# Linear attention and a mixture of experts on one core: paired x blocks, moved weight loads, split output queues and a new front order

## The chip, the core and the metric

The kernel runs on one core of a Trainium2 chip. A core has five engines with instruction streams of their own: TensorE (PE) multiplies matrices, VectorE (DVE) and ScalarE (ACT) do elementwise work and empty PSUM, GpSimd (POOL) does a little elementwise work, and SyncE (SP) issues DMAs. DMAs are issued from the streams of SP, ACT and POOL, each a queue of its own. Every engine works through its instructions in the order in which they were written, so an instruction that waits holds all behind it. The metric is the device time of one execution in microseconds, lower is better; the result is the median of several runs.

## The reference

```
phi(x) = elu(x) + 1
kv  = einsum('bhsd,bhse->bhde', phi(k), v);  z = sum_s phi(k)
att = (phi(q) @ kv) / (phi(q) . z + 1e-6)          # 8 batches, 8 heads, 576 x 64, float32
x   = att as [4608, 512]                           # tokens x (heads * 64)
P   = exp(x @ w_gate - max), then 8 rounds of normalising rows and columns   # 4608 x 8 experts
out = sum over e of P[:, e] * (relu(x @ w1[e]) @ w2[e])     # w1: 512 x 1024, w2: 1024 x 512
```

Every token goes through all eight experts, so the experts make most of the work. The weights and inputs are float32 in memory; the kernel computes in float16 with float32 sums.

## The kernel before, in words

**Attention.** There are 16 attention steps, numbered n = 2b + g: batch b, and half g of its heads (`att`, L361 on). Each loads k, q and v (L382), each 576 KB of float32: k as float32 (and the very first q), the other q and all v as float16. ScalarE takes exponentials (L393, L456), VectorE makes phi with two passes each (L397, L401, L459, L463). PE makes kv (L422), transposes q (L448), and multiplies for denominator and numerator (L479). ScalarE takes the logarithm of the denominator and the exponential of minus that (L492, L497), VectorE multiplies and writes `xT` (L507). The k loads share three buffers with the first q. With `sp` true a load goes to SP's queue: in the kernel before, these are k of n = 0, k of n = 1 and q of n = 0; all the other loads go to POOL's.

**Expert 0** follows behind the attention while it runs. Tokens are cut in nine blocks ("units") of 512. Layer 1 of the first units is plain (`layer1`, L696), layer 2 too (L979); later units use a scheme of seven products for a 2 x 2 split instead of eight, which needs sums of the weights' quarters (`combos`: W at L1021, T at L1035) and of the inputs' quarters (S, L1066).

**x blocks.** For experts 1 to 7 the seven input quarters and their sums are written to memory once (`xd`, `x_blocks`) and read back for every expert (`x_load`, L783) to ten slots `xs`. The units are grouped in `SUBS`: unit 0 is single, then come four pairs. A pair's block has 256 KB, a single unit's 128 KB; in the kernel before each block takes a slot of its own. Seven slots exist from the closing of the front on, the other three only when xT's space is given up (`f_xclose`), after the last reader of `xT` and after the gate's P is done. The order of loading is that of `ORD`: blocks 1, 5, 6, 3, 2, 7, 4.

**Experts 1 to 7** run as 63 steps, each half a pair's layer 1 or all of unit 0's (`l1_half`, `pair`, L801) beside the layer 2 of an earlier unit (`layer2`, L1095). VectorE and, for one group in seven, ScalarE and GpSimd add P times the result to `acc` (L1126, L1133, L1136). PSUM banks are few, so PE waits for these evictions when they are late.

**Weights** come through POOL's queue (`load_w`, L313), with two buffers each for w1 and w2: expert 0's in two pieces (`parts=2`), the others' w1 as two DMAs of 512 KB and w2 as one of 1 MB. A limit of eight outstanding loads is kept on that queue (`p_sw`).

**The end.** For expert 7, `out_dma` (L956) writes each finished tile of 128 tokens as two halves of 64 partitions. Unit 8 is done by `last`, with its own order of tiles.

**What sets the order.** All instructions are recorded as tasks with costs, dependencies, priorities and buffer groups (`_Plan.add`). `_Plan.run` then goes through a simulated time and writes them out engine by engine. `_FRONT` fixes the first part by hand: a list of task numbers with a letter for the engine (p PE, a ACT, d DVE, g POOL, s SP, m a DMA under way, n none), from the start until some way into expert 1's share; after it the planner picks by earliest start and priority. At the beginning 46 warm-up matmuls (L598) stand in PE's stream between the first useful ones.

Of the kernel before, what the change touches and what calls it, by code (L numbers as in the profile page):

```python
# [17 lines left out]
class _Plan:  # L18
# [35 lines left out]
    def run(self):  # L54
# [33 lines left out]
        while left:  # L88
            best = None
            if fixed:  # L90
                t, e = fixed.pop()
                t = self.t[t]
# [3 lines left out]
            for e, lst in avail.items() if best is None else ():  # L96
                te = None
                for t in lst:
                    r = slot(t)
                    if r is None:  # L100
                        continue
                    s = at(e, t, r)
                    if te is None or s < te:
                        te = s
                if te is None:
                    continue
                pick = None
                for t in lst:
                    r = slot(t)
                    if r is not None and at(e, t, r) <= te + 1e-9 and (pick is None or (t["prio"], t["id"]) < (pick["prio"], pick["id"])):  # L110
                        pick = t
                if best is None or te < best[0]:
                    best = (te, e, pick)
# [26 lines left out]
1n 2p 3p 4p 0g 80g 5p 52g 6p 48s 49m 7p 8p 9p 10p 11p 12p 13p 14p 15p 16p 17p 76s 50s  # L140
51m 18p 19p 54a 20p 21p 22p 61n 23p 108n 78g 24p 25p 26p 27p 28p 29p 30p 31p 55d 62a 56d 63d 64d
65p 77m 82a 83d 84d 66a 53m 57n 58p 59a 60a 32p 33p 34p 35p 36p 79m 89n 90a 91d 67p 68a 81m 595n
85n 86p 92d 120g 118g 119m 37p 122g 148g 146g 109g 38p 87a 88d 121m 125d 69p 70a 71a 123m 39p 93p 94d 111g
40p 41p 74p 75d 42p 149m 124a 126d 150g 174g 176g 95p 96a 43p 44p 72p 45p 110m 73d 147m 127n 131n 133d 132a
159n 46p 97p 47p 98a 99a 113n 134d 202g 178g 128p 112m 114g 151m 206g 175m 160a 129d 161d 130d 135p 136d 177m 187n
596p 597p 100p 116g 101d 137p 138a 162d 179m 115m 207m 203m 598p 599p 139p 140a 102p 153d 103d 152a 154d 155n 141a 204g
205m 232g 106g 234g 233m 235m 163p 164a 600p 602p 604p 601d 603d 104g 605d 117m 156p 157a 606p 608p 158d 181d 144p 145d
180a 182d 236g 609a 165p 188a 166a 105m 237m 610p 607a 142p 143d 260g 261m 612p 167p 189d 190d 168a 169a 613d 183n 184p
185d 186d 191p 192d 611a 618p 172p 173d 262g 614p 615d 193p 194a 208a 170p 171d 107m 245n 263m 209d 210d 215n 217d 211n
632n 216a 616p 195p 633p 196a 634d 635p 636a 197a 246a 238a 218d 212p 213d 214d 637p 638d 219p 220d 200p 639p 292g 290g  # L150
247d 248d 201d 239d 240d 221p 222a 291m 641p 640a 642a 264g 617p 223p 293m 224a 225a 265m 198p 199d 624d 267d 241n 619p
249p 250d 273n 266a 242p 243a 244d 626a 620p 643p 320g 294g 318g 346g 274a 268d 275d 276d 348g 322g 321m 251p 252a 303n
226p 621p 644a 297d 227d 253p 622p 645p 319m 349m 296a 254a 228p 304a 646a 229d 298d 305d 269n 230p 270p 231a 271d 255a
277p 350g 376g 295m 278d 272a 374g 323m 375m 377m 331n 332a 333d 406g 647p 648a 258p 259d 666p 279p 280a 628a 256p 306d
257d 623p 281p 282a 283a 299n 665n 300p 630d 307p 301d 308d 378g 302d 324a 667a 347m 379m 359n 351m 360a 325d 361d 334d
668p 651p 309p 310a 284p 285d 326d 362d 669a 670p 653p 311p 312a 286p 287d 327n 654p 380a 335p 336d 328p 661a 313a 329d
330a 288p 289a 381d 560d 404g 407m 405m 493g 671d 353d 652p 352a 408g 460g 494m 314p 315d 337p 659a 338a 561d 672p 674p
675d 673a 339p 316p 354d 317d 355n 387n 389d 388a 491g 382d 390d 676p 678p 409m 461m 469s 462g 340a 677a 492m 463m 341a
470s 356p 363p 364d 464g 465m 471s 500s 417n 357a 679a 358a 501s 680p 410a 342p 343d 365p 366a 649p 562d 419d 344p 345d
553d 367p 368a 418a 681a 699p 383n 384p 385a 411d 386d 554d 369a 495g 496m 502s 563s 432g 433m 434g 435m 655p 391p 392a  # L160
372p 373d 412d 701p 656p 370p 371d 420d 497a 393p 394a 445n 413n 650p 414p 698n 700a 436g 415d 498d 499d 416d 702a 657a
395p 503g 396a 564m 555d 556s 558s 397a 663a 438a 437m 703p 682p 421p 400p 705p 684p 422d 439d 423p 704a 424a 401d 446a
447d 440d 574d 575d 557m 685p 398p 399d 683p 576d 577s 578m 559m 441n 476n 477a 425p 706d 426a 707p 708a 448d 692d 442p
443a 444a 709p 449p 478d 690d 450d 427a 508n 509a 479d 567d 688p 689p 451p 710a 428p 429d 581d 568d 582d 452a 569d 570s
572s 565s 571m 566m 686p 711p 453p 696a 454a 455a 466a 430p 431d 583d 713p 584s 579s 585m 588g 589n 480p 481d 510d 504n
592n 573m 687p 456p 457d 511d 712d 402p 505p 739n 403a 506a 593g 714d 507a 694d 467d 468d 512p 740p 590g 458p 459d 472n
741a 580m 513a 742p 744p 591m 514p 515a 473p 735d 474d 475d 736d 516p 517a 518a 719p 720p 482p 483a 743a 519p 520d 727d
721p 484p 485a 521p 745d 522d 737d 746p 722p 486a 747a 489p 715p 490d 738d 487p 488d 551n 731d 778d 1009s 1011s 748p 749a
729a 750p 752p 751a 779d 732d 780d 523p 524a 754p 552p 716p 733d 526d 753a 755a 786p 717p 723a 787a 525n 527p 586s 1013s
1015s 781s 800p 718p 790p 756d 734d 792p 785n 1017s 725a 791a 1010m 587m 788p 793a 801a 789a 760p 761a 836d 757d 837d 758d  # L170
528d 838d 783s 1019s 1021s 839s 796p 529d 759d 784m 804p 805a 806p 807a 766p 767a 782m 794p 802p 803a 810p 795d 797d 811d
762p 763a 840m 1022m 1014m 808p 809d 1001d 770p 771d 768p 530p 1002d 769d 531d 798p 812p 799a 813a 772p 773a 844p 845a 764p
894d 814d 846p 847a 848p 850p 858p 852p 843n 849a 859a 765a 851a 532d 815d 816d 820p 860p 818p 861a 866p 895d 853d 817d
819a 864p 854p 865a 533p 896d 897s 855d 867d 534d 824p 825a 868p 869d 862p 863a 535d 856p 857a 821a 828p 829d 870p 871a
902p 903a 826p 822p 952d 872d 827d 953d 1003d 823a 954d 955s 1012m 1018m 956m 873d 1004d 906p 830p 831a 908p 916p 876p 841s
899s 957s 909a 912p 536p 874d 537d 918p 901n 907a 875d 917a 922p 920p 594m 878p 898m 877a 919a 921a 904p 905a 923a 882p
883a 880p 881a 879a 926p 924p 538d 886p 913d 914p 927d 925d 887d 915a 910p 539p 540d 911d 884p 960p 961a 888p 889a 928p
962p 963a 959n 966p 964p 541d 885d 929a 930d 967a 965a 968p 969d 542p 543d 974p 975a 934p 970p 978p 976p 931d 971d 1020m
1016m 958m 980p 935a 977a 979a 981a 940p 972p 973a 936p 984p 544d 545p 982p 941a 932d 546d 983d 1023p 1024a 938p 985d 1025p
547d 1029p 986p 944p 937a 939a 1026a 945d 1030a 1031p 1027p 842m 900m 987a 548p 1033p 946p 947a 1028a 933d 942p 549d 1034d 1035p  # L180
1037p 1038a 988p 550d 1000n 625a 1036a 1032d 1513n 943d 1005d 1006d 1051s 1053s 1055s 1057s 1052m 1039p 989p 1043p 1054m 1514g 1056m 990p
1040a 629a 1044a 691d 1045p 1041p 996d 1047p 1065p 1048d 1042a 693d 1059s 1066a 631a 1061s 1060m 1058m 1062m 1063s 1147s 1149s 1064m 1067p
991p 1068a 1046d 1049p 992p 1071p 1072a 1073p 1069p 1074d 1075p 1050a 951a 1076d 774d 997d 1121d 1070a 993p 1077p 1079p 1081p 1078a 695d
1080a 1082a 994p 1085p 1087p 1083p 1086a 627a 1007d 1122d 728a 1084a 1089p 1088d 1123d 1090d 998d 1093p 1094a 1095p 1148m 1096a 1515m 995p
999a 1091p 1092a 1099p 1101p 1097p 1008d 1100a 1124d 1102d 1125p 1126a 1127p 1129d 1128d 1130p 1103p 1104d 1133a 1134g 1098a 1135p 1138p 1151s
1152m 1516n 1150m 1136d 1137d 1105p 1106a 1107p 1109p 1108a 1110a 1153s 1155s 1154m 1141p 1142d 1143d 1113p 1115p 1114a 1139d 1111p 1117p 1161p
1163p 1144p 834d 1116d 1118d 1119p 1157s 1131a 1112a 1156m 1162a 1167p 660a 1159s 1140d 662d 1146d 1145d 1269s 1271s 1164a 1169p 1165p 1120a
1189d 1168a 1193p 1195p 891a 1158m 1190d 1191d 1194a 664a 1198p 1201a 1166a 892a 658a 1171p 697d 1203p 1160m 1202g 1197d 1196d 1192d 1206p
1172d 1173p 1132g 1199a 1519d 1200g 1175p 1177p 1204d 1205d 1174a 1176a 1209p 1181p 1178a 1183p 1179p 1207d 1517g 1170d 1211d 1208d 1210d 1182a
# [27 lines left out]
def kernel(  # L217
# [553 lines left out]

    xst_of, xse_done, sx_users = {}, [], []

    n_load = [0]

    def x_load(d, blk, prio):
        gr = S_.grp(p_xs)
# [533 lines left out]
```

## Time and profile before

| | us |
|---|---|
| median of 3 runs | 959.46 (959.14 to 959.91) |
| profiled execution | 959.16 |
| its span in the trace | 957.4 |
| PE busy | 945.6 |
| DVE busy | 774.1 |
| ACT busy | 581.8 |
| POOL busy | 146.3 |
| granted PE clock, share of full | 0.999 |
| DMA busy, mean of 16 engines, 0 to 22.4 us | 1.03 of the window |
| the same, 120 to 183 us | 0.49 |
| the same, 183 to 190 us | 0.96 |

Times are counted from the span's start. A line of instructions has start, duration, engine, line of the kernel, operation, and output and inputs by the program's names; in brackets stands how long the engine was idle before it and what released it. SPq, ACTq and POOLq are DMA issues. A wait line has the waiting engine and operation, the releaser, the total, the number and the longest. The chain that ended last follows the work back from the last instruction; its lines have start, duration and what ran. The end of a matmul is modelled, and neighbours overlap, so two matmuls are told apart by their starts.

### The profile page before, as it was taken

To read this page: it belongs to the slowest core of one execution; us is meant where nothing else is said; L and a number is where in the kernel's file an instruction comes from. 1 tells how busy PE (TensorE), PEld (TensorE's weight loads), DVE (VectorE), ACT (ScalarE), POOL (GpSimd) and SP (SyncE) were. 2 spreads that over 40 slices of the span, in tenths; PEclk is the share of its full clock that TensorE was granted. 3 is DMA by queue.
4 is the path that set the end of the run, shared out by engine and by line. 5 is a ranking of instruction groups with operands and counts; after the bars stand their busy time and mean duration, and the time that the engine had idled before them with its cause. 6 is when DMAs were issued, how large, how long until landed. Compare 5 with 4: busy or idle time off the path is not lost.

```text
span 957.4 us, 18335 instructions
## 1 busy us (share of the span) xinstructions
PE 945.6 (99%) x7008; PEld 651.5 (68%) x7008; DVE 774.1 (81%) x1499; ACT 581.8 (61%) x1034; POOL 146.3 (15%) x208
## 2 busy tenths in 40 slices
PE   8999999999999999999999999999999999999997
PEld 4565588666677666766677666766667666776665
DVE  6998999778987888778888888878887888877775
ACT  6899766676655555555555555555555555555552
POOL 6432000001111111111111111111112111111110
PEclk9999999999999999999999999999999999999999
DMA  9998663525136222652217321552217422125544
GB/s 246 262 238 208 157 163 95 154 78 122 61 75 147 77 79 61 176 121 77 63 48 163 89 78 61 139 115 71 76 49 170 116 79 61 56 78 165 165 134 132
DMA packets 87908, 112.65 MB, mean 118 GB/s; under 512 B 7436, under 2 KB 51468, under 8 KB 87820
## 3 DMA queue, kind: packets, MB, share of 16 engines
q1 hardware_dynamic: 63708, 76.77, 26.0%
q0 software_dynamic: 23712, 34.19, 19.2%
q8 instruction: 55, 0.90, 0.4%
q10 hardware_dynamic: 400, 0.52, 0.2%
q14 instruction: 33, 0.27, 0.1%
HBM read 119.69 MB, written 17.69 MB: 143 GB/s over the span
## 4 chain that ended last, share of the span: by engine, by line
PE 90%; DMA 4%; ACT 3%; DVE 2%; issue 1%; SPq 0%; POOL 0%; DVEq 0%
PE ye L1095 36%; PE hq L801 24%; PE R L801 12%; PE Zye L801 6%; PE Zye L1095 6%; PE ye L979 2%; PE hq L696 1%; DMA hb<-in_q_dram 1%; DMA w<-in_moe_w_dram 1%; DMA kin<-in_q_dram 1%; ACT eq L456 1%; DMA xs<-xd 1%; ACT rden L492 1%; PE kv_ps L422 1%; DVE xT L507 0%
## 5 line engine op out<-in xcount | busy, mean ns | idle before, releaser
L1126 DVE SCALAR_TENSOR_TENSOR acc<-ye,P_sb,acc 128x256 f32<-128x256 f32 x620 | 267.2, 479 | 126.6 <-PE ye L1095 124.5
L1095 PEld LDWEIGHTS <-S 128*128 128x128 f16 x1984 | 194.0, 98 | 46.6 <-DVE S L1066 0.2
L1095 PE MATMUL ye<-T,S 128*128 128x256 f16 x1488 | 192.8, 273 | 0.0
L1136 POOL TENSOR_TENSOR acc<-acc,st 128x256 f32<-128x256 f32 x124 | 88.9, 737 | 632.7 <-ACT st L1133 632.7
L1095 PEld LDWEIGHTS <-hb 128*128 128x128 f16 x1584 | 155.0, 98 | 42.7 <-issue 0.8
L801 PEld LDWEIGHTS <-W 128*128 128x128 f16 x1248 | 122.1, 98 | 86.8
L832 ACT ACTIVATE hb<-hq 128x512 f16<-128x512 f32 x134 | 80.0, 597 | 138.6 <-PE hq L801 133.8
L801 PE MATMUL hq<-xs,W 128*128 128x512 f16 (+1 forms) x560 | 150.0, 358 | 0.0
L801 PE MATMUL R<-xs,W 128*128 128x512 f16 (+1 forms) x560 | 150.0, 358 | 0.0
L801 PE MATMUL hq<-xs,w 128*128 128x512 f16 (+1 forms) x560 | 139.8, 358 | 1.3 <-DMA xs<-xd 1.3
L801 PEld LDWEIGHTS <-w 128*128 128x128 f16 x936 | 91.5, 98 | 60.9 <-issue 1.8
L829 ACT ACTIVATE hb<-Zye 128x512 f16<-128x512 f32 x134 | 80.1, 598 | 37.9 <-PE Zye L801 37.8
L835 DVE CUSTOM_DVE_ANT_0 hb<-hq,sx 128x512 f16<-128x512 f32 x126 | 86.6, 687 | 16.8 <-PE hq L801 16.8
L1133 ACT ACTIVATE st<-Zye,P_sb 128x256 f32<-128x256 f32 x124 | 52.5, 471 | 75.6 <-PE Zye L1095 75.6
L822 ACT COPY sx<-hq 128x512 f32<-128x512 f32 x126 | 73.6, 584 | 37.1 <-PE hq L801 37.1
L835 DVE CUSTOM_DVE_ANT_0 hb<-R,sx 128x512 f16<-128x512 f32 x126 | 86.4, 685 | 8.9 <-ACT sx L822 8.9
L818 ACT COPY Zye<-hq 128x512 f32<-128x512 f32 x134 | 77.8, 581 | 21.0 <-PE hq L801 20.8
L1066 DVE TENSOR_TENSOR S<-hb 128x1024 f16<-128x1024 f16 x124 | 84.9, 685 | 4.8 <-ACT hb L832 4.7
L801 PE MATMUL Zye<-xs,w 128*128 128x512 f16 (+1 forms) x280 | 75.0, 358 | 0.0
L826 ACT COPY sx<-R 128x512 f32<-128x512 f32 x126 | 74.4, 591 | 0.0
L1095 PE MATMUL ye<-w,hb 128*128 128x256 f16 x528 | 68.4, 273 | 0.5 <-DVE acc L1126 0.5
L1095 PE MATMUL Zye<-w,hb 128*128 128x256 f16 x528 | 68.4, 273 | 0.0
(119 smaller groups left out, 981.4 us busy)
## 6 DMA issues: line engine op xcount, KB each, us to landing
xs<-xd SPq DMA_DIRECT2D x196, 256.0 KB, 3.8
out_dram<-acc SPq DMA_DIRECT2D x67, 128.0 KB, 2.4
w<-in_moe_w_dram POOLq DMA_DIRECT2D x16, 512.0 KB, 7.9
kin<-in_k_dram POOLq DMA_DIRECT2D x14, 576.0 KB, 8.2
w<-in_moe_w_dram POOLq DMA_DIRECT2D x7, 1024.0 KB, 9.6
xs<-xd SPq DMA_DIRECT2D x49, 128.0 KB, 2.6
vv<-in_v_dram POOLq DMA_DIRECT2D x16, 288.0 KB, 7.2
hb<-in_q_dram POOLq DMA_DIRECT2D x15, 288.0 KB, 7.8
```

What stands on the lines that cost most here:

```text
L801: nc.tensor.matmul(dst_[:, p, :] if parts == 2 else dst_.rearrange("p a b -> p (a b)"), lhsT=lhs(p, c), rhs=blk[i](c), start=(first and p ...
L818: nc.scalar.copy(out=Zt[1], in_=gX["tile"])
L822: nc.scalar.copy(out=gs2["tile"], in_=gX["tile"])
L826: nc.scalar.copy(out=gs5["tile"], in_=gR["tile"])
L829: nc.scalar.activation(out=dst(0, 0), in_=Zt[1], func=AF.Relu)
L832: nc.scalar.activation(out=dst(1, 0), in_=gX["tile"], func=AF.Relu)
L835: nc.vector._custom_dve(TENSOR_ADD_SAT, out=out_, in0=ps, in1=sb, s0=3.0e38, s1=0.0)
L1066: nc.vector.tensor_tensor(out=Sx[:, i], in0=a0, in1=a1, op=op)
L1095: nc.tensor.matmul(bank(g_)[:, s, :], lhsT=lhs(s, kk), rhs=rhs(kk), start=(new and s == 0 and kk == 0), stop=(kk == 3), skip_group_check=True)
L1126: nc.vector.scalar_tensor_tensor(out=dst(), in0=bank(g_)[:, s, :], scalar=P_sb[:, gg, e:e + 1], in1=dst(), op0=ALU.mult, op1=ALU.add)
L1133: nc.scalar.mul(out=gst["tile"], in_=bank(g_)[:, s, :], mul=P_sb[:, gg, e:e + 1])
L1136: nc.gpsimd.tensor_tensor(out=dst(), in0=dst(), in1=gst["tile"], op=ALU.add)
```

## The change

1. A single unit's x blocks go two to a slot, so that its seven blocks take four slots; a paired unit's still take one each.
2. Expert 2's w1 waits in the plan for the x loads of step 1 (the first pair's, for expert 1) to have landed.
3. Only n = 0's k and q go to SP's queue, q first; k of n = 1 goes to POOL's.
4. For unit 7 as well as unit 8, the second half of each output tile is issued by ScalarE and not by SP.
5. In the planner, DMA tasks are picked by readiness and not by priority, and some DMA costs are changed.
6. `_FRONT` is a new list up to task 1842. Among other things, 27 warm-up matmuls and not 30 stand before the first useful one, w1 of expert 0 is loaded in two places (after k of n = 3, and after v of n = 3), and on POOL w1 of expert 1 comes before its w2. From PE's 1,611th matmul on, PE's order is the same in both kernels.

```diff
-                    if r is not None and at(e, t, r) <= te + 1e-9 and (pick is None or (t["prio"], t["id"]) < (pick["prio"], pick["id"])):
+                    if r is not None and at(e, t, r) <= te + 1e-9 and (
+                            pick is None or (t["ready"] if e == "dma" else t["prio"], t["id"]) <
+                            (pick["ready"] if e == "dma" else pick["prio"], pick["id"])):
...
-1n 2p 3p 4p 0g 80g 5p 52g 6p 48s 49m 7p 8p 9p 10p 11p 12p 13p 14p 15p 16p 17p 76s 50s
-51m 18p 19p 54a 20p 21p 22p 61n 23p 108n 78g 24p 25p 26p 27p 28p 29p 30p 31p 55d 62a 56d 63d 64d
+50s 51m 108n 61n 1n 113n 2p 48s 49m 3p 4p 5p 6p 7p 8p 9p 10p 11p 12p 13p 14p 15p 16p 17p
+18p 62a 63d 54a 0g 19p 20p 21p 22p 23p 24p 25p 26p 27p 64d 55d 28p 65p 78g 79m 89n 52g 53m 56d
...
-            sp = wide and b == 0
+            sp = n == 0 and wide
...
-    def x_load(d, blk, prio):
-        gr = S_.grp(p_xs)
-        i = n_load[0] % NXS
-        n_load[0] += 1
-
-        def fn(_):
-            gr["tile"] = xs_t[i]
-            nc.sync.dma_start(out=xs_t[i][:, :, 0:len(SUBS[d])], in_=xd[d][:, blk])
+    def x_load(d, prio):
+        gx = {}
+        dbl = len(SUBS[d]) == 2
+        for m, (blk, b) in enumerate(ORD.items()):
+            h_ = 0 if dbl else m % 2
+            if h_ == 0:
+                gr = S_.grp(p_xs)
+                i = n_load[0] % NXS
+                n_load[0] += 1
+
+            def fn(_, gr=gr, h_=h_, i=i, b=b):
+                gr["tile"] = xs_t[i]
+                nc.sync.dma_start(out=xs_t[i] if dbl else xs_t[i][:, h_], in_=xd[d][:, b] if dbl else xd[d][:, b, :, 0])
...
-            st["x"] = {i: x_load(d, b, un) for i, b in ORD.items()}
+            st["x"] = x_load(d, un)
+            if n == 1:
+                first_x.extend(t for _, t, _ in st["x"].values())
...
-                eng = nc.scalar if g == NG - 1 and half == 1 else nc.sync
+                eng = nc.scalar if g >= NG - 2 and half == 1 else nc.sync
...
-                w_t[e] = load_w1(e, prio=float(e), deps=w_t[e - 1][1][1:]) + load_w2(e, prio=float(e), deps=w_t[e - 1][3][1:])
+                w_t[e] = load_w1(e, prio=float(e), deps=w_t[e - 1][1][1:] + (first_x if e == 2 else [])) + load_w2(e, prio=float(e), deps=w_t[e - 1][3][1:])
```

## The prediction

> **What bounds the kernel now.** I read the busy shares first, then who PE waited for, then the chain that ended last, and then the time lines of the three places where PE is not streaming.
>
> ```profile
> span 957.4 us, 18335 instructions
> PE 945.6 (99%) x7008; PEld 651.5 (68%) x7008; DVE 774.1 (81%) x1499; ACT 581.8 (61%) x1034; POOL 146.3 (15%) x208
> ...
> PE hq L801 <- DMA xs<-xd: 1.3, 1, 1.3
> PE att L448 <- ACT rden L492: 1.2, 2, 0.6
> PE att L448 <- DVE tq L463: 0.8, 2, 0.6
> ```
>
> PE is busy 99% of the span, and the change removes no matmul, so only time in which PE has no useful work can be won. A busy PE hides some of that (the 46 warm-up matmuls count as work), so I counted it in the trace: the useful matmuls at their start-to-start times (216 ns for 512 columns, 109 for 256, 122 for 288, 41 for 192, 56 for 128, 25 for 8) make 924.2 us. The time PE has lost against that is 17.2 us when the first layer-1 matmul starts at 22.4, 19.5 at 40, 24.7 at 180, 26.2 at 190 and 27.8 at 940; 5.5 more follow the last matmul. From 190 to 940 nearly nothing is lost. Three places remain.
>
> ```profile
> 11.47 10.81 DMA w<-in_moe_w_dram
> ...
> 179.68 5.63 DMA xs<-xd
> ```
>
> In the chain, the start runs through DMA: expert 0's first weights are on their way for 10.8 us. Much later one load of x blocks takes 5.63 us.
>
> ```profile
> 10.63 0.68 PE L448 MATMUL att<-ident,tq 128*128 128x128 f16 x9
> ...
> 16.32 1.16 ACT L497 ACTIVATE rden<-rden 128x1152 f32<-128x1152 f32 x1
> ...
> 22.42 1.02 PE L696 MATMUL hq<-xT,w 128*128 128x512 f16 x4 [0.20 <-DMA w<-in_moe_w_dram]
> ...
> 174.51 0.62 POOL L313 DMA_DIRECT2D w<-in_moe_w_dram  x1 [60.48 <-PE hq L801]
> ...
> 185.32 0.59 PE L801 MATMUL hq<-xs,w 128*128 128x512 f16 x2 [1.32 <-DMA xs<-xd]
> ...
> 950.45 0.88 DVE L1126 SCALAR_TENSOR_TENSOR acc<-ye,P_sb,acc 128x256 f32<-128x256 f32 x2
> ...
> 952.19 0.48 DVE L1200 SCALAR_TENSOR_TENSOR acc<-hq,P_sb,acc 128x256 f32<-128x256 f32 x1 [0.39 <-PE hq L1191]
> ```
>
> The time line shows the start (first attention matmul at 10.63, first layer-1 matmul at 22.42, waiting for weights), the one stall in the middle (1.32 us before expert 1's second unit) and the end: the last eviction is over at 952.67, 4.7 us before the span ends.
>
> **The end: late halves on ScalarE's queue.** The trace has SP issue its last output DMAs at 950.96, 951.51, 952.20, 952.80, 953.51 and 954.22, some 0.6 us apart: SP is the queue that ends last, 1.5 us behind the last data, and the final wait falls 2.26 us after the last issue (956.48). Unit 7's eight outputs now split four and four. Walked with the same 0.6 us steps, SP and ACT each issue at 950.35, 950.96, 951.51, 952.15 and 952.80. That moves the end from 954.22 to 952.80: 1.4 us won. ACT computes nothing after 943.6, and its DMAs stand behind its last multiply, so nothing waits for them. Bounds: 1.55 (no queue at all behind 952.67), and 0.6 (one step only, if two queues at once slow each landing). I take 1.4.
>
> **The middle: x blocks two per slot, expert 2's weights behind them.** A single unit's seven blocks filled seven of ten slots, all that are there before xT's space closes (178.8 us). Now they fill four, so the second unit's first three blocks are loaded before that; the unit's first three matmul groups (blocks 1, 5, 6) have their data. Expert 2's w1, issued at 174.51 and 176.21 in front of these loads, moves behind them. The 1.32 us stall should go. Next late are blocks 3 and 2, which still wait for the closing. In the new order seven matmul groups (four of 0.86, three of 0.43) stand between the closing and block 3's first use, 4.7 us; a block's load takes 3.8 us at the median and 0.35 to issue: covered. If it took 5.63 again, 1.3 of cover is missing. Bounds: 1.3 won to 1.3 lost; I take 1.3 won, since the load that made 5.63 us is gone from there.
>
> Expert 2's w1 is now issued on POOL after unit 1's adds, which end at 216.8, and not at 174.5. Two halves landed 9.7 us after the first issue at 174.51, and 1 MB issued at 216.72 took 10.1. So it lands near 226.7. Its first reader on DVE now stands behind unit 2's second pair of evictions (226.86 plus 0.88 = 227.7): 1 us of cover, at no cost. Behind it DVE holds PE's accumulator evictions, but the next idle there is 2.10 us, so a late landing costs nothing up to 3 us. All of this moves together if PE is earlier. w2 follows with a longer cover still. The 49 single loads of 128 KB stay 49 issues on SP; that each now fills half a slot in one piece I cost at nothing, since PE waits for none of them after 190.
>
> **The front.** The landing events stand 1.40 to 1.45 us apart from 9.15 to 33 us, load after load in order of issue, so DMA is the clock of the start and a place in the queue is worth 1.4 us. Before, eleven loads (three on SP: k, k, q) stand ahead of w1, whose first half lands at 22.28. Now ten do: 20.9. The second k, formerly on SP and landed at 6.0, is the fifth load and lands near 10.5; the second v is the seventh, near 13.4 (it was 9.15). w1's second half stands behind q and v of the fourth pair: about 26.6 instead of 24.82. On POOL the second k adds one issue of 0.72 us; w1's issue waited there until 10.80 for buffers, but lands 10 us later behind the row, so the issue does not set it. SP only loses an issue.
>
> The first q is now first on SP and lands near 4.6 instead of 8.59, but PE stands behind 27 warm-up matmuls instead of 30: the first transposes start 3 x 0.216 = 0.65 us earlier, at 10.0. From there I walked ACT, DVE and PE in their new orders with the spacings of the trace (exponentials 1.06 us apart, logarithms 0.65, DVE passes 0.68). qpT is copied at 10.55, the second k's exponential follows at 11.6 and the first logarithm at 12.7 (14.31 before). The reciprocal's exponential comes at 15.1 (16.32 before): 1.2 us ahead. The second pair gives part of it back: its kv waits for order and v until 14.75 (13.52), and its qpT copy has moved from DVE (0.76) to ACT (1.12). The third kv comes at 19.9 (20.05), and the first layer-1 matmul stands behind a num matmul that needs a kvz copy on ACT, behind the second pair's exponential (20.2 to 21.25). It starts at 21.9 against 22.42, with 0.24 us more work done: 0.76 ahead. At 27 us, where layer 1 waits for w1's second half, the walk is 0.9 ahead. After 40 us PE is fed by ACT and DVE at 90% and 91% (71.92 and 72.81 of 80 us), and the two orders are alike in kind; I take no further change and 0.7 won. Bounds: 2.5 won (1.4 from w1's place and about half of the 2.9 us of listed PE waits) and 3.0 lost (1.2 from the second kv, 1.8 from w1's second half).
>
> **Sum.** 1.4 + 1.3 + 0.7 = 3.4 us. The planner's new costs and its pick of DMA tasks by readiness act through the order alone. The profiled execution took 959.16 with a span of 957.38, so 955.8; it stood 0.3 under the median 959.46, so 956.1.
>
> A rule that speaks against the change stands in the Trainium skill, "SBUF — State Buffer", section "SBUF: two separate sides": DMAs issued from GpSimd starve while VectorE runs in a mode that takes the shared port. The trace has GpSimd's issues of v at 0.70 to 1.11 us, median 0.72, beside a DVE busy 80%, so by this row the harm is 0.4 us at most. By the rule the front's gain would be lost, and the sum would be near 2.7.
>
> **Rivals.** (1) *GpSimd is held back*, the rule's case. If the second k's issue waits out one DVE pass of 0.76 us, the whole row of loads moves by that, and the front gains nothing: 956.8. Against it: the issues beside DVE passes took 0.87 instead of 0.72. (2) *The stall stays*, because blocks 3 and 2 come late after a later closing (the last Sinkhorn matmul stands ten groups further back): 957.4. (3) *The front loses 1.2*, the second kv's delay, and nothing brings it back: 958.0. (4) *The front wins its 2.5* because w1 was the true gate: 954.3. (5) *Slower:* the new order does not fit the chip between 22 and 180 us. One engine waiting in order holds the next; PE's waits there, beyond 0.23 us of loading per kv, are 4.3 us now. With the end's and the middle's 2.7 won and the front at nothing, the kernel is slower by over 0.2% from 4.6 more on. At 4.3 to 8.6 more, middle 6.4: 963.2. For it: ACT and DVE have 10% to spare there. Against it: the order is of the same make as one that fits.
>
> **How the numbers follow.** Forecast 0.45, (1) 0.04, (2) 0.08, (3) 0.14, (4) 0.13, (5) 0.16. A change under 0.2% (1.9 us) can't be told from none. Faster: forecast, (1), (2) and (4), 0.70; same: (3), 0.14; slower: (5), 0.16. The range leaves out (5) and the edges: low 953.8 (best front and 1.5 at the end), high 960.0 (a front that loses 1.9 and a stall that stays).
>
> **What would show it.** The last SP output issue within 0.3 us of the last eviction, and 4.7 us after that eviction shrinking to 3.3; no wait of PE for xs near 184; w1's first half landing near 20.9 and the first layer-1 matmul near 21.9; lost time at 180 near 24.0 (24.7 now). The prediction is wrong if lost time at 180 exceeds 26, if a wait for xs stands elsewhere, or if DVE waits for w near 226.

## The result, and the profile after

| | us |
|---|---|
| before, median of 16 runs | 959.62 (959.07 to 960.44) |
| changed kernel, median of 16 runs | 961.80 (960.02 to 963.20) |
| ratio | 1.0021 (95% interval 1.0014 to 1.0029) |
| predicted | 956.1 (953.8 to 960.0), chance of slower 0.16 |
| profiled execution of the changed kernel | 963.20, span 961.4 |

The change makes the kernel slower by 0.2%, where 0.35% faster was forecast. The profiled execution is the slowest of its sixteen, so its trace shows more loss than a typical run has. PE's two longest waits in the changed kernel (their total, number and longest):

```profile
PE R L816 <- DMA xs<-xd: 1.8, 1, 1.8
PE Zye L816 <- DMA xs<-xd: 1.6, 1, 1.6
```

The wait for x blocks near 184 us is gone; two others for x blocks are new. They stand close together, 47 us later. The time lines of PE and of the two queues that load there (start, duration, engine, line, operation; in brackets the idle time and what ended it):

```profile
224.05 0.93 POOL L318 DMA_DIRECT2D w<-in_moe_w_dram  x1
...
225.77 5.52 SPq L793 DMA_DIRECT2D xs<-xd  x7
...
230.78 0.59 PE L816 MATMUL hq<-xs,W 128*128 128x512 f16 x2
233.16 0.60 PE L816 MATMUL R<-xs,W 128*128 128x512 f16 x2 [1.79 <-DMA xs<-xd]
235.42 1.01 PE L816 MATMUL Zye<-xs,w 128*128 128x512 f16 x2 [1.65 <-DMA xs<-xd]
236.22 1.91 PE L1112 MATMUL ye<-w,hb 128*128 128x256 f16 x8
237.93 1.91 PE L1112 MATMUL ye<-T,S 128*128 128x256 f16 x8
239.64 1.92 PE L1112 MATMUL Zye<-w,hb 128*128 128x256 f16 x8
241.34 0.64 PE L816 MATMUL hq<-xs,W 128*128 128x512 f16 x2
241.82 1.04 PE L1112 MATMUL ye<-T,S 128*128 128x256 f16 x8
```

GpSimd issues expert 2's w2, 1 MB, at 224.05; SP issues the seven x blocks from 225.77 on, 1.75 MB. PE waits twice. Then three groups of eight matmuls take 1.71 us each from start to start, and the same kind takes 0.88 at 241.82: PE runs at half its rate from 235.4 to 241.3. The windows from 230 to 240 us of the changed kernel and of the kernel before (columns: length, busy time of PE, weight loads, DVE, ACT and POOL with counts, granted PE clock, DMA share, GB/s):

```profile
230.00:240.00 10.00, 6.56 (x31) 3.78 (x30) 3.64 (x8) 2.63 (x5) 0.00 (x0) 0.73 0.78 224
```

```profile
230.00:240.00 10.00, 10.00 (x72) 6.85 (x70) 9.80 (x20) 5.88 (x11) 1.36 (x2) 1.00 0.53 179
```

Before, PE is full there at clock 1.00. After, the clock is 0.73. The DMA view of that stretch (KB of one issue, median us from issue to landing), after and before:

```profile
xs<-xd SPq DMA_DIRECT2D x7, 256.0 KB, 9.3
w<-in_moe_w_dram POOLq DMA_DIRECT2D x1, 1024.0 KB, 12.4
```

```profile
xs<-xd SPq DMA_DIRECT2D x7, 256.0 KB, 4.5
w<-in_moe_w_dram POOLq DMA_DIRECT2D x1, 1024.0 KB, 10.1
```

In the kernel before, w2 was issued at 216.72 and had landed at 226.82, ahead of the first block's issue (228.52):

```profile
216.72 0.93 POOL L313 DMA_DIRECT2D w<-in_moe_w_dram  x1
```

In the changed kernel it is still on its way while the blocks are loaded, and they take twice as long.

PE's lost time, counted as in the prediction:

| at | before | after | won so far |
|---|---|---|---|
| first layer-1 matmuls, 22 us | 17.2 | 16.8 | 0.5 |
| 40 | 19.5 | 18.9 | 0.6 |
| 180 | 24.7 | 23.2 | 1.5 |
| 190 | 26.2 | 23.3 | 2.9 |
| 230 | 26.3 | 23.6 | 2.7 |
| 250 | 26.3 | 30.3 | -4.0 |
| 940 | 27.8 | 31.2 | -3.4 |

Up to 230 us the changed kernel is 2.7 us ahead. Between 230 and 250 it loses 6.7: 4.2 in and around the waits and 2.5 in 24 matmuls of 0.213 us where 0.109 is full speed.

### The profile page after: what moved, and what is told of

It is laid out like the page before. It is cut to its first block, busy times and chain, and to the rows that moved or that the text cites. A ratio compares the mean times of both kernels' runs of the same rounds, so it can differ in the third digit from the quotient of the medians.

```text
span 961.4 us, 18327 instructions
## 1 busy us (share of the span) xinstructions
PE 948.1 (99%) x7008; PEld 652.8 (68%) x7008; DVE 776.4 (81%) x1500; ACT 582.8 (61%) x1033; POOL 143.4 (15%) x209
## 4 chain that ended last, share of the span: by engine, by line
PE 95%; DVE 2%; ACT 1%; DMA 1%; issue 0%; DVEq 0%
PE ye L1112 36%; PE hq L816 24%; PE R L816 12%; PE Zye L1112 6%; PE Zye L816 6%; PE ye L996 3%; PE hq L701 3%; PE yw L603 1%; PE kv_ps L427 1%; DMA xs<-xd 1%; PE att L484 1%; PE num_ps L484 1%; PE att L453 1%; PE hq L1208 0%; PE att L529 0%
```

## The experiments

Theory: w2's new place (behind the first add of the next unit) makes its transfer collide with the x blocks, and without that the change would gain what was forecast. The rival: the blocks are late by themselves, by late slots or late issue.

**1. w2 early, in the changed kernel.** Nothing but GpSimd's order changes.

```diff
-... 1200g 1514g 1515m 1244d ...            (w1 of expert 2)
-... 1302a 1517g 1518m 1254g ...            (w2 of expert 2, then an add)
+... 1200g 1514g 1515m 1517g 1518m 1244d ...
+... 1302a 1254g ...
```

> The changed kernel with one move on GpSimd: expert 2's w2 is issued right behind its w1, ahead of the next add, and not behind it (224.05 us before). Theory A, collision: w2's 1 MB then lands near 224, before the x blocks issued at 225.8; these land in under 5 us and not in 9.3, PE no longer waits for xs at 231 and 233 (3.8 us), and the half-speed matmuls behind these waits (2.5 us) go too. Lost time between 220 and 250 falls from 6.7 us to under 0.5, and the time from 961.8 to 956.2 (955.5 to 957.0). Theory B, the blocks are late for another reason (late free slots, or their issue on SP): the two waits stay, 961 to 962.

Measured: 955.67, ratio 0.9965 (0.9952 to 0.9977). The same stretch:

```profile
230.00:240.00 10.00, 10.00 (x72) 6.87 (x71) 9.29 (x20) 5.58 (x11) 0.95 (x1) 1.00 0.23 81
```

PE is full, the clock is 1.00, and the blocks land in 4.1 us. w2, now third in its queue, was issued at 213.04 and landed at 226.12, 2 us later than thought but early enough: its last packet moved at 225.82, the blocks' first at 225.95. Lost time from 220 to 250 is 0.04 us. One position in one queue separates 961.8 from 955.7: theory A.

**2. w2 late, in the kernel before.** The mirror image: `1517g 1518m` moved behind the add `1254g` in the old list.

> The kernel before with one move on GpSimd: expert 2's w2 is issued one add later, near 227.4 us and not at 216.72, so that it stands just ahead of the x blocks issued from 228.5 on, as in the changed kernel. Theory A, collision: these blocks take about 9 us and not 4.5, PE waits 3 to 4 us for xs between 233 and 240, with up to 2.5 us more if matmuls run at half speed afterwards: 959.5 becomes 962.5 to 966. Theory B, the wait comes from other parts of the change: 959.5 stays, within 0.5.

Measured: 963.0, ratio 1.0041 (1.0027 to 1.0054); w2 issued at 227.19, the blocks from 228.32 on:

```profile
235.30 0.60 PE L801 MATMUL R<-xs,W 128*128 128x512 f16 x2 [1.38 <-DMA xs<-xd]
237.59 0.59 PE L801 MATMUL Zye<-xs,w 128*128 128x512 f16 x2 [1.69 <-DMA xs<-xd]
238.02 1.03 PE L1095 MATMUL ye<-w,hb 128*128 128x256 f16 x8
```

```profile
xs<-xd SPq DMA_DIRECT2D x7, 256.0 KB, 9.8
w<-in_moe_w_dram POOLq DMA_DIRECT2D x1, 1024.0 KB, 12.9
```

The same two waits appear in a kernel with none of the other changes. So w2's place alone is enough. Here the matmuls behind the waits run at full speed (0.87 us for eight).

**3. w2 later still, in the changed kernel:** `1517g 1518m` behind `1254g`.

> The changed kernel with w2 of expert 2 issued one add later still, near 229.4 us, when four of the seven x blocks are already issued. Theory A, what counts is which transfer stands first in the DMA engines: w2's head start of 1.7 us is gone, the first blocks land in about 4 us, and the two waits of 3.8 us in sum shrink to below 1.5: 957 to 959. Theory B, w2 and the blocks share the bandwidth whatever their order: the waits stay near 3.5 us: 960.5 to 962.

Measured: 956.56, ratio 0.9965 (0.9951 to 0.9979). w2 was issued at 229.21, behind six of the seven blocks:

```profile
xs<-xd SPq DMA_DIRECT2D x7, 256.0 KB, 4.6
w<-in_moe_w_dram POOLq DMA_DIRECT2D x1, 1024.0 KB, 12.6
```

No wait is left, better than theory A said. So w2 may come 11 us earlier or 5 us later than in the changed kernel: only the place just ahead of the blocks costs. Its first reader (T on VectorE) starts at 253.4 us in experiment 1, 260.9 in the changed kernel and 254.1 here, far behind the landings (226.1, 236.5, 241.9).

**4. w1 early, pairing left.** Expert 2's w1 goes back to where it was before, w2 takes its place, and `first_x` is dropped from the dependencies:

```diff
-load_w1(e, prio=float(e), deps=w_t[e - 1][1][1:] + (first_x if e == 2 else []))
+load_w1(e, prio=float(e), deps=w_t[e - 1][1][1:])
-... 1000n 1057s ...     ... 1094a 1513n 1099p ...    ... 1200g 1514g 1515m 1244d ...
+... 1000n 1513n 1514g 1515m 1057s ...   ... 1094a 1099p ...   ... 1200g 1517g 1518m 1244d ...
```

> The changed kernel with expert 2's w1 issued early, near 175 us as in the kernel before (it no longer waits for unit 1's x blocks), and its w2 in w1's place behind the second add (near 213). So of the middle's two parts only the pairing of blocks is left. Theory A, the pairing alone removes the wait at 184: no wait of PE for xs there, lost time from 180 to 190 under 0.3 us, and none near 231, since w2 is early: 956.2 (955.5 to 957.0). Theory B, w1's place was what counted: PE waits 1 to 2.6 us for xs near 184 again: 957.2 to 958.8.

Measured: 956.12, ratio 0.9967 (0.9955 to 0.9978). No wait for blocks near 184: lost time from 180 to 190 is 0.08 us. w2, issued at 212.87, landed at 222.34.

**5. Pairing alone, in the kernel before:** the new `x_load` and `view`, with the old list and the old dependencies.

> The kernel before with the paired x blocks alone (w1 early at 175, everything else as before). Theory A: unit 1's first three blocks are loaded ahead of the closing of xT's space, and the wait of PE for xs near 184 (1.49 us in the profiled run, 0.6 and 0.8 in the two other profiles with that place unchanged) goes: lost time from 180 to 190 under 0.2 us, 958.0 to 959.0 (959.6 before). Theory B: the blocks then collide with w1's two DMAs, and the wait stays or moves: 959.2 to 960.5.

Measured: 958.69, ratio 0.9991 (0.9982 to 1.0000); lost time from 180 to 190 is 0.01 us. The two last runs agree: pairing removes the wait by itself, and w1's move was not needed for it. (w1's move without the pairing was not run.) In the changed kernel's order it is w1's move that filled GpSimd's place behind the second add, so that w2 slid behind the next one. The wait itself was smaller than the profiled run showed: lost time from 180 to 190 is 1.48 in the kernel before, but 0.59 and 0.79 in experiments 2 and 6, which have that place unchanged.

**6. The split output alone, in the kernel before:**

```diff
-                eng = nc.scalar if g == NG - 1 and half == 1 else nc.sync
+                eng = nc.scalar if g >= NG - 2 and half == 1 else nc.sync
```

> The kernel before with the output change alone: unit 7's second halves on ScalarE's queue. Theory A, what the changed kernel's trace shows: the last issue comes 1.1 us earlier against the last eviction, but the last transfer lands 2.8 us after its issue on ScalarE's queue and not 2.3 as on SP's, and the closing is 0.4 longer; the end stands 4.5 us behind the last eviction and not 4.7, so 959.4 (959.0 to 959.7). Theory B, the prediction: 1.4 us won, 958.1.

Measured: 958.87, ratio 0.9993 (0.9984 to 1.0002). Between the two theories, and the interval holds both no gain and the predicted gain.

**7. The split output undone, in the kernel of experiment 1** (the same line back):

> The first run's kernel (w2 early) with the output change undone: only unit 8's second halves go to ScalarE's queue. Theory A: the split output is worth what its issues show, 1.1 us: the last issue comes 1.5 us behind the last eviction and not 0.5, and the time rises from 955.7 to 956.8 (956.4 to 957.2). Theory B: the landings at the end swing by as much as is won, and no difference shows in the time: 955.5 to 956.0.

Measured: 956.85, ratio 0.9968 (0.9955 to 0.9980); by ratios a loss of 0.3 us that the intervals do not separate from none. The traces say more. Both kernels have lost 24.5 us at 940 and end their last eviction at 949.4. Undone, and with the split:

```profile
947.71 4.44 SPq L973 DMA_DIRECT2D out_dram<-acc  x6
```

```profile
947.74 2.75 SPq L973 DMA_DIRECT2D out_dram<-acc  x4
947.10 3.42 ACTq L973 DMA_DIRECT2D out_dram<-acc  x5
```

SP's issues end at 952.15 undone; with the split the last of both queues ends at 950.52. The spans are 954.8 and 953.7, 1.1 us apart. Over all profiles, the time from the end of the last eviction to the end of the span is 4.2 to 4.6 us with the split in six and 5.4 in one (experiment 4), and without it 5.3 to 5.4 in three (experiments 2, 5, 7) and 4.7 in the kernel before. So these traces put the split at about 1 us, with an outlier on either side, and the profile that the prediction went by is one of them. The times of this experiment and of experiment 6 alone do not separate it from nothing.

**8. The second k back on SP, in the kernel of experiment 1:** `sp = wide and b == 0`, and `76g` becomes `76s`.

> The first run's kernel (w2 early) with the second k back on SP's queue, as its third load. Theory A, GpSimd's queue starts late: with two loads on SP the landings of the changed kernel have a hole of 0.75 us between the second (6.17) and the third (8.35); a third load on SP fills it, the row behind comes 0.7 earlier (w1's first half at 21.1 and not 21.8), and PE has lost up to 0.7 us less at 40 us: 955.0 to 955.7. Theory B, the first q and v on GpSimd's queue lose as much as the second k gains, or PE is not set by the row: no difference, 955.4 to 956.2.

Measured: 956.70, ratio 0.9971 (0.9960 to 0.9982), so no gain: the median lies above the ranges of both theories, and the difference to experiment 1 lies within the intervals. Theory A falls in the trace too: the third landing came at 9.86 and not earlier than 8.35, so the hole behind the second (6.09) grew to 3.8 us. The first v landed behind it, at 11.49 and not 9.34, and PE waited 2.06 us for that v before the first kv. Lost time at 40 us was 21.2 against 18.2 in experiment 1. w1's first half landed nearly alike (21.04 and 20.81), so this loss did not come through w1's place in the row.

**9. Thirty warm-up matmuls ahead again, in the kernel of experiment 1:** `29p 30p 31p` moved behind `28p`.

> The first run's kernel (w2 early) with 30 warm-up matmuls and not 27 ahead of the first useful one, as in the kernel before. Theory A: PE's own order sets the start: the first transposes come 0.65 us later, and so does all that follows: lost time at 40 us 0.65 higher, 956.1 to 956.6. Theory B: the chain over ScalarE and VectorE or the landings set the start; the three matmuls are hidden again by 40 us: 955.4 to 956.0.

Measured: 957.10, above the ranges of both theories; the ratio, 0.9972 (0.9962 to 0.9983), is not separated from the 0.9965 with 27. In the trace the first transposes start at 9.48 and not 8.69, and lost time at 40 us is 18.7 and not 18.2. But in the five profiles of the new order with 27 (the changed kernel, experiments 1, 3, 4 and 7) the transposes start anywhere from 8.49 to 9.95, and this lost time varies by about 1 us, so one trace does not decide between the theories.

## Why the prediction was wrong

**The step that failed** is the last of the middle part: "w2 follows with a longer cover still". It looked at w2's own reader and found it covered, which was right (T at 260.9 us, w2 landed at 236.5). It did not ask what else is in the DMA engines while w2 is on its way, and so put w2's effect on the x blocks at nothing. For w1 the prediction had such a term: it counted the block load of 5.63 us, behind w1, as gone once w1 moved. But w1 took w2's place behind the second add on GpSimd, and w2 had to wait out the next add: it was issued at 224.05 us and not at 216.72, just ahead of the x blocks at 225.77. The sum lacks a term of 5 to 6 us: 961.80 against 955.67 by medians, 0.56% or 5.4 us by ratios. In the profiled run it is 4.2 us in and around two waits and 2.5 us at half the clock.

The profile of before had the same delay, unread. With w1's two halves on their way (until 184.21), the blocks issued from 178.81 on moved their first packet only 3.2 us later; over the 70 or so times that SP's queue was idle when a block was issued, the median is 0.94 us. w1 itself did as forecast or better: it landed at 220.87 and not 226.7, and VectorE did not wait for it. The rival for "slower" was another one: it put the loss into waits between 22 and 180 us, where the changed kernel gained. One listed sign was the right one, "if a wait for xs stands elsewhere".

**The rest of the sum was nearly right in total, in part by luck.** Without the collision the kernel takes 955.67, forecast 956.1, but two terms were too large and the third was too small. By terms:

- *The middle, 1.3 predicted.* Right in mechanism: the pairing removes the wait (0.08 us left). The size was taken from one profile of a wait that varies; alone it gave 0.9 us (959.56 to 958.69, an interval that just reaches no gain). The other half, w1 behind the blocks, was costed as part of the gain; the wait goes without it (experiments 4 and 5), and with it the kernel is not clearly faster (955.67 against 956.12).
- *The end, 1.4 predicted.* The issues came nearly as walked, SP's last at 957.07 and ScalarE's at 957.36, 0.2 and 0.5 us behind the last eviction, against 1.5 before. The 4.7 us after the last eviction became 4.5 in the profiled run and not 3.3: the last landing took 2.8 us from its issue and not 2.3, and the closing 0.4 more. That profile of before had an end shorter than the others without the split; the pair of traces in experiment 7 gives 1.1.
- *The front, 0.7 predicted, about 2.4 measured.* Lost time at 180 us is 22.4 to 23.6 in the five profiles with the new order (mean 22.9; the changed kernel, experiments 1, 3, 4 and 7) and 24.7 to 25.9 in the four with the old (mean 25.4; the kernel before, experiments 2, 5 and 6). At 22 us the means stand 0.8 apart and at 40 us 1.4. Two steps were too small. The first transposes were moved by three warm-up matmuls, 0.65 us, from 10.63. But in the profile of before they stood behind q and not behind the warm-ups; its thirty warm-ups ran until q was ready, so that no wait was listed. In the three other profiles of the old order they ran faster and q came later (VectorE begins on it at 9.44 and not 8.62 in experiment 5), and the wait shows, here from that experiment:

```profile
11.45 0.68 PE L448 MATMUL att<-ident,tq 128*128 128x128 f16 x9 [1.97 <-DVE tq L463]
```

  The new order has q first, and its transposes start at 8.49 to 9.95 without a wait. The second step is "after 40 us ... I take no further change": another 1.0 us is won between 40 and 180. No single wait of more than 0.2 us stands there in either kernel, and which part of the order wins it stays open.
- *The walk of the front* held else: the second k's exponential at 11.30 (11.6), the reciprocal's at 14.87 (15.1), the third kv at 19.95 (19.9), the first layer-1 matmul at 22.20 (21.9). Only the row of loads was off: w1's first half at 21.82 and not 20.9. GpSimd's first load landed 2.2 us behind SP's second and not 1.4, and one later landing is 1.3 us late (19.61, 2.7 us behind the load before). In the four other profiles of the new order it is 20.81 to 21.29. Nor is the row as even as the prediction reads it: in the profile of before, w1's four pieces stand 1.2 to 1.3 us apart, 2.0 behind the load ahead of them, and not 1.40 to 1.45.
- *GpSimd held back,* the rule from the Trainium skill ("SBUF — State Buffer", section "SBUF: two separate sides"), did not show here. In the changed kernel GpSimd's issues of k, q and v in the first 60 us took 0.72 us at the median and 0.85 at the longest, nearly all of them beside a VectorE instruction. In the other profiles a few took 1.0 to 1.2 us, so some 0.4 us more, the bound of the prediction. Its 0.87 us for issues beside VectorE passes does not come out of the profile of before: there the mean is 0.77. The second k's own issue, 0.73 us, met no VectorE instruction and says nothing on the rule.
- *The low edge of the range,* 953.8, is taken from the profiled execution and not from the median, from which the same gains of 5.3 us lead to 954.2. Nothing hangs on it.

The lowest median is that of experiment 1: 955.67, 0.35% under the kernel before and some 0.6% under the changed one. Experiments 3 and 4 (ratios 0.9965 and 0.9967) are not separated from it.

## What to carry to other kernels

A load that is moved needs two questions: when is it read, and which transfers will it be in the engines with. When one load takes a place in an in-order queue, look at where the one that stood there goes; here the slip of the second load cost more than all the gains. Look in the trace for a place where such transfers meet already: in the profile of before it stood at 178.81 us. Take the size of a wait from several profiles, and do not read "no wait listed" as "not waiting" where filler work such as warm-up matmuls stands in front.

## What the runs showed of the hardware

**Blocks issued behind a weight load start late, then share the engines.** In the changed kernel SP issued the first block at 225.77. Until 229.60, 3.8 us later, GpSimd's queue (q0) alone moved packets; then both did, and in experiment 1 SP's (q1) had the engines for itself. The queues' packets, MB and share of the engines' time, in the changed kernel from 225.77 to 229.60 and from 231 to 234 us, and in experiment 1 from 229 to 231:

```profile
q0 software_dynamic: 536, 0.55, 110.8%
```

```profile
q0 software_dynamic: 289, 0.29, 58.7%
q1 hardware_dynamic: 294, 0.53, 53.9%
```

```profile
q1 hardware_dynamic: 417, 0.76, 103.6%
```

Sharing, the blocks move 0.53 MB in 3 us, some 180 GB/s; alone 0.76 MB in 2 us, 380 GB/s. In the Trainium skill, "DMA: Bandwidth & Descriptors", section "Queues, rings and completion order", it says that each DMA engine takes turns between the queues that have work, a packet at a time. From 231 to 234 us the trace agrees, with 289 and 294 packets; in the 3.8 us before, the blocks had been issued and none of their packets moved. In the nine other profiles where w2 is not just ahead of the blocks, their first packet comes 0.9 to 1.0 us after the issue; in experiment 2 it comes after 3.7. In experiment 3, with the blocks ahead, w2's own first packet comes 2.7 us after its issue, against 1.6 in the kernel before. So in these traces the load issued second starts late; why is not shown. The first two blocks landed 7.4 and 9.2 us after their issues, against 2.8 and 2.9 in experiment 1.

**Two short waits, then PE at half its clock.** After 1.79 and 1.65 us of idle with 0.43 us of work between them, PE ran at half speed for 6 us, which cost some 2.5 us more; the granted clock was 0.50 from 234.6 to 241.4 us. After 1.38 and 1.69 us in the profile of experiment 2 it stayed at 1.00. Over the 16 runs of the changed kernel the mean granted clock was 0.996 in six (962.16 to 963.20 us), 0.997 or 0.998 in seven, and 0.999 in three (960.02, 960.30 and 962.01). The means of the first and the last group are 962.7 and 960.8 us, so much of the spread of 3 us goes with the clock. One run of experiment 2 had 0.997, and it was its slowest (965.58); no run of a kernel without the two waits is below 0.998. The Trainium skill's page "TensorE: Matmul & The Clock Gate", section "What's actually happening", has PE fall to half its rate after an idle window of about 3.4 us; here no single wait was longer than 1.8 us, and the two together made 3.4. What decides between the two outcomes was not tried.
